# Attention and a gated feed-forward layer on one core: five of seven score slots transposed by DMA, q loaded in 1 KB packets, sums inverted before they are transposed

## The chip, the core and the metric

The kernel runs on one core of a Trainium2 chip. Its engines are TensorE (PE, with its weight loads shown as PEld), VectorE (DVE), ScalarE (ACT), GpSimd (POOL) and SyncE (SP), which here issues every DMA; 16 DMA engines move the data. The metric is device time in microseconds. Three runs of the kernel before gave a median of 922.18 us (921.71 to 923.18). A difference of 0.2% (1.8 us) is about what such a measurement can tell from no change.

## The reference

Eight batches of twelve heads, 448 tokens, head size 64. `q` and `k` are normalised by their root mean square and a gain, then come softmax attention and, per batch, a feed-forward layer: a 768 to 1024 product, relu, a convolution over three neighbouring tokens, a sigmoid gate, and a 1024 to 768 product.

```python
    q_n, k_n = (rmsnorm(q, g_q), rmsnorm(k, g_k))
    scores = scale * np.matmul(q_n, k_n.transpose(0, 1, 3, 2))
    scores = scores - np.max(scores, axis=-1, keepdims=True)
    attn = np.exp(scores)
    attn = attn / (np.sum(attn, axis=-1, keepdims=True) + 1e-09)
    return np.matmul(attn, v).astype(np.float32)
    ...
    h = np.maximum(x @ w_in, 0.0)
    for k in range(K):
        conv_out += conv_w[k][None, None, :] * hp[:, k:k + S, :]
    gate = 1.0 / (1.0 + np.exp(-conv_out))
    return (h * gate @ w_out).astype(np.float32)
```

## The kernel before

The work is cut into 48 **pairs** of heads, six to a batch. A pair has 2 x 448 = 896 query rows, cut into seven **slots** of 128; slot 3 lies across both heads. For a pair, q, k and v come in by one DMA each (`load_k`, `load_q`, `v_load`). Squares, their sums (`square`, `square_sum`) and a Newton iteration (`rsqrt`) give the norms, `apply_rms` applies them. K is turned by PE and split into two fp16 halves (`qk_transpose`, `qk_hi`, `qk_lo`); q likewise up to pair 7 and by a DMA transpose from pair 8 on (`x_cast`, `x_rest`, `x_turn`).

Scores (`scores`, L600) are three fp16 products of the halves for each slot. Slots are computed in `GROUPS`: two slots of different heads go side by side on the two halves of PE's rows (`HALF`), the slot across both heads takes the whole array with a masked copy of q (`qz`). `soft_max` (DVE, L604) and `soft_exp` (ACT, L614) give the unnormalised powers `e` and, as an accumulator, the row sums `rsum`.

The powers P have to be turned before they meet v. There are two ways. On the **raw** way four fp32 transposes on PE (`p_transpose`, L651) put a slot into PSUM, `p_evac` (a copy that shows as L78) brings it to `PT`, and `pv` multiplies it in fp32 with `v` (L723). On the **cast** way `p_hi` and `p_lo` split the slot into two fp16 halves in one of three buffers `ph`, `p_turn` (L643) is a DMA transpose into `PT`, and `pv` multiplies in fp16 with the split v, `vp`, in three products (L732). `nd(n)` is the number of slots on the cast way: none up to pair 7, four (slots 0, 6, 1, 5) from pair 8 on.

v is scaled by a power of two per batch (`v_scaled`, L696, in place, for every pair), then cast (`v_hi`, `v_lo`). The row sums go `sum_transpose` (PE, L666), `sum_evac` (DVE, L671, adds 1e-9), `sum_inverse` (DVE, L663, a reciprocal of 7 x 128), `sum_store` to DRAM (SP, L676) and two `sum_load`s (SP, L682), one for each head, which spread a head's 448 values over 64 partitions of `rB`. `x_scale` (DVE, L741) multiplies the product in PSUM with `rB`, and `x_hi` and `x_lo` split it into the fp16 halves `x` of the feed-forward layer. Once a batch has its six pairs, `in_part` (L806), `in_relu`, `in_conv`, `in_tanh`, `in_gate`, `in_hi`, `in_lo` and `out_part` (L883) follow, interleaved with the next batches' attention.

**What sets the order.** Every step is planned with a due time (`at`), and a planner lays the steps out before the program is built. It knows for each step which engines may do it and an assumed cost (`options`), what it needs (`needs`), how many buffers there are (`BUFS`), and picks step after step by the earliest start and the due time. `PH` holds the due times' parameters and the extra delay that a second choice of engine has to beat. The result is one fixed order on each engine, and an instruction that waits holds up everything behind it on its engine. So any edit to costs, steps or `PH` moves nearly every instruction. In the first 150 us or so the weights are also loaded, converted and split (`convert`, L210 to L218, `split`, `rest`).

Of the kernel before, what the change touches and what calls it, by code (L numbers as in the profile page):

```python
# [49 lines left out]
def tile_attention_moe(ctx: ExitStack, tc, q, k, v, g_q, g_k, w_in, conv_w, w_out, out):  # L50
# [41 lines left out]
    def move(e, dst, src):  # L92
# [10 lines left out]
        rB=2, vacc=2, vsc=4, cwb=3, s=4, t=2, m=4, rd=2, rsum=2, rT=2, mx=10, ph=3, vp=2,  # L103
# [60 lines left out]
    warm = const.tile([P, 1], F32, name="warm")  # L164

# [401 lines left out]
    SLOTS = (0, 6, 1, 5, 2, 4, 3)  # L567
    GROUPS = ((0, 1), (2, 3), (4, 5), (6,))
# [4 lines left out]
    def nd(n):  # L573
        return 0 if n < PH["n1"] else 2 * PH["dg"]
# [14 lines left out]
    def scores(n, g):  # L589
# [29 lines left out]
    def inside(n, j):

        return PH["ein"] and j < nd(n)

    def powers(n, j):
        return bank("s", (n, j))[:, :S] if inside(n, j) else old("e", (n, j))

    def p_hi(n, j):
# [28 lines left out]
    def p_evac(n, j):  # L655
        c = SLOTS[j] - nd(n) // 2
# [4 lines left out]

    def sum_inverse(n):
        nc.vector.reciprocal(old("rT", n), old("rT", n))  # L663
# [6 lines left out]
    def sum_evac(n):  # L670
        nc.vector.tensor_scalar(  # L671
            new("rT", n, [NS, P], F32), bank("t", ("r", n))[:NS, :P], 1e-9, None, op0=ALU.add
# [5 lines left out]
    def sum_load(n, h):  # L678
        if h == 0:
            new("rB", n, [P, S], F32)  # L680
        row = old("rd", n).rearrange("t p -> (t p)")[h * S : (h + 1) * S]
        queue("rb").dma_start(  # L682
            old("rB", n)[HALF[h]], row.unsqueeze(0).to_broadcast([64, S])
# [7 lines left out]
    def pvs(n):  # L691
        return (*range(0, NB, PV_STEP), *(range(NB, NB + 3) if nd(n) else ()))

    def v_scaled(n):
        v = old("v", n).rearrange("p h t d -> p (h t d)")
        elementwise(on["v_scaled", n]).tensor_scalar(  # L696
            v, v, old("vsc", n // NP)[:PB, 1:2], None, op0=ALU.mult
        )
# [38 lines left out]
    def x_place(n):  # L737
        return bank("m", ("v", n))[:, :S] if PH["xin"] else old("rB", n)

    def x_scale(n):  # L740
        nc.vector.tensor_tensor(x_place(n), bank("m", ("v", n))[:, :S], old("rB", n), op=ALU.mult)  # L741

    def x_hi(n):
        copy(on["x_hi", n], new("x", n, [P, 2, S], F16)[:, 0], x_place(n))

    def x_lo(n):
        xt = old("x", n)
        binary(on["x_lo", n], xt[:, 1], x_place(n), xt[:, 0], ALU.subtract)

    def plan_attention(n):  # L750
# [197 lines left out]
    def prepare():  # L948
# [3 lines left out]
        nc.vector.memset(ones, 1.0)  # L952
# [605 lines left out]
```

## Time and profile before

| | |
|---|---|
| median of three runs | 922.18 us (921.71 to 923.18) |
| the profiled execution, its own time | 925.0 us |
| its span in the trace | 923.2 us |
| mean granted TensorE clock | 0.972 |
| PE busy | 849.0 us |
| DVE busy | 730.2 us |
| ACT busy | 667.4 us |
| POOL busy | 627.3 us |
| DMA queue, share of 16 engines | 62.1% |

Busy time of an engine is the time in which at least one of its instructions runs. Matmuls are pipelined and overlap in the trace, so what a group of them costs is read from where the next group starts. The other 1.8 us of the profiled execution lie outside the span. DMA-issuing instructions are not counted as busy time of SP.

### The profile page before, as it was taken

How to read it: one execution, taken by the hardware profiler on the slowest of the kernel's cores; microseconds unless marked ns; L12 is line 12 of the kernel's file. 1: busy time of each engine (PE TensorE's matmuls, PEld its weight loads, DVE VectorE, ACT ScalarE, POOL GpSimd, SP SyncE). 2: the span in 40 equal slices, each digit the busy share in tenths (PEclk: the TensorE clock that was granted, in tenths of full speed). 3: DMA queues.
4: the chain of work that ended last, by engine and by line, in shares of the span. 5: the costliest groups of instructions: out<-in, count | busy, mean ns of one | idle time of the engine just before them, and what ended most of it. 6: DMA issues, size and time to landing. Idle time of an engine off the chain costs nothing.

```text
span 923.2 us, 18519 instructions
## 1 busy us (share of the span) xinstructions
PE 849.0 (92%) x6430; PEld 508.7 (55%) x6430; DVE 730.2 (79%) x1336; ACT 667.4 (72%) x1525; POOL 627.3 (68%) x705
## 2 busy tenths in 40 slices
PE   1686687998999999999999999999999999999998
PEld 0343344555656566556665566566655666566554
DVE  6998987999788887798798976898789876893330
ACT  3677776887688776788688877787788867885441
POOL 2396887787699768668688857777778755872120
PEclk9897787999999999999999999999999999999999
DMA  8934432376885878556976588568696695455001
GB/s 212 259 96 126 122 113 63 89 135 117 185 147 130 156 152 170 123 117 124 187 148 139 115 182 168 95 135 164 150 170 126 119 175 120 84 94 112 18 18 52
DMA packets 296878, 120.18 MB, mean 130 GB/s; under 512 B 258048, under 2 KB 293200, under 8 KB 296784
## 3 DMA queue, kind: packets, MB, share of 16 engines
q1 hardware_dynamic: 296784, 119.00, 62.1%
q8 instruction: 50, 0.82, 0.4%
q14 instruction: 44, 0.36, 0.1%
HBM read 56.65 MB, written 11.18 MB: 73 GB/s over the span
## 4 chain that ended last, share of the span: by engine, by line
PE 67%; DVE 18%; DMA 5%; ACT 4%; issue 2%; SPq 2%; POOL 2%; DVEq 0%; ACTq 0%; POOLq 0%
PE bank L883 19%; PE bank L806 19%; PE bank L600 9%; PE bank L723 7%; PE bank L651 6%; PE bank L732 4%; DMA rB<-rd 3%; PE bank L462 2%; DVE rT L663 1%; DMA v<-in_v_dram 1%; DVE st L365 1%; DVE wo L214 1%; POOL sq L90 1%; DVE vacc L528 1%; SPq L643 1%
## 5 line engine op out<-in xcount | busy, mean ns | idle before, releaser
L806 PE MATMUL bank<-x,wi 128*128 128x448 f16 x1152 | 241.9, 354 | 0.3 <-ACT e_(8_0_1731 L614 0.3
L883 PE MATMUL bank<-wo,gring 128*128 128x384 f16 (+1 forms) x1056 | 205.4, 327 | 0.7 <-DVE c_(4_7_8185 L839 0.3
L806 PEld LDWEIGHTS <-wi 128*128 128x128 f16 x1152 | 110.2, 98 | 99.8 <-issue 14.7
L883 PEld LDWEIGHTS <-gring 128*128 128x128 f16 (+1 forms) x1056 | 101.8, 99 | 62.7 <-issue 11.0
L78 ACT COPY PT<-bank 112x512 f32<-112x512 f32 x166 | 96.6, 586 | 42.9 <-PE bank L651 41.9
L600 PE MATMUL bank<-kT,qT 64*128 64x448 f16 x864 | 107.1, 370 | 1.2 <-ACT qT L78 0.6
L90 POOL TENSOR_TENSOR sq<-qkf,st 112x512 f32<-112x512 f32 x79 | 87.5, 1125 | 17.6 <-DVE st L387 15.6
L723 PE MATMUL bank<-PT,v 112*64 112x192 f32 (+1 forms) x768 | 88.8, 374 | 1.7 <-ACT PT L78 1.3
L90 POOL TENSOR_TENSOR x<-rB,x 128x448 f16<-128x448 f32 x48 | 51.5, 1073 | 47.5 <-ACT x L78 36.4
L723 PEld LDWEIGHTS bank<-PT,v 112*64 112x64 f32 x768 | 51.5, 138 | 34.5 <-issue 18.1
L600 PEld LDWEIGHTS <-qT 64*128 64x128 f16 x864 | 34.8, 97 | 49.4 <-issue 28.2
L365 DVE TENSOR_REDUCE st<-sq 112x16 f32<-112x1024 f32 x48 | 57.9, 1207 | 3.7 <-ACT sq L357 3.6
L732 PE MATMUL bank<-PT,vp 112*64 112x256 f16 x960 | 59.2, 273 | 0.0
L696 POOL TENSOR_SCALAR v<-v,vsc 112x512 f32<-112x512 f32 x35 | 57.6, 1649 | 1.9 <-DVE vsc L200 0.9
L732 PEld LDWEIGHTS <-vp 112*64 112x64 f16 x960 | 53.0, 110 | 2.6
L741 DVE TENSOR_TENSOR rB<-bank,rB 128x448 f32<-128x448 f32 x48 | 29.7, 619 | 29.4 <-DMA rB<-rd 20.7
L491 POOL COPY qz<-qT 64x128 f16<-64x128 f16 x88 | 33.2, 378 | 28.3 <-DMA qT<-qkf 17.2
L462 PE MATMUL bank<-ident,sq 112*128 112x112 f32 x224 | 33.6, 276 | 18.8 <-POOL sq L90 18.7
L90 POOL TENSOR_TENSOR vp<-v,vp 112x512 f16<-112x512 f32 x39 | 46.6, 1195 | 2.8 <-ACT vp L78 1.6
L883 PE MATMUL bank<-wo,wi 128*128 128x384 f16 (+1 forms) x192 | 46.9, 326 | 0.0
L663 DVE RECIPROCAL rT<-rT 7x128 f32<-7x128 f32 x48 | 44.9, 935 | 0.7
L90 POOL TENSOR_TENSOR qkf<-sq,qkf 112x512 f16<-112x512 f32 x29 | 35.0, 1208 | 13.8 <-ACT qkf L78 7.2
(2235 smaller groups left out, 2101.6 us busy)
## 6 DMA issues: line engine op xcount, KB each, us to landing
qkf<-in_k_dram SPq DMA_DIRECT2D x48, 224.0 KB
qkf<-in_q_dram SPq DMA_DIRECT2D x48, 224.0 KB
v<-in_v_dram SPq DMA_DIRECT2D x48, 224.0 KB
rB<-rd SPq DMA_DIRECT2D x96, 112.0 KB
wo<-in_moe_w_in_dram SPq DMA_DIRECT2D x12, 512.0 KB
gring<-in_moe_w_out_dram SPq DMA_DIRECT2D x16, 384.0 KB
PT<-ph SPq DMA_TRANSPOSE x160
rd<-rT SPq DMA_DIRECT2D x48, 3.5 KB
```

Of the source, the lines that this page charges most:

```text
L78: (nc.scalar.copy if e == "ACT" else elementwise(e).tensor_copy)(dst, src)
L90: elementwise(e).tensor_tensor(dst, a, b, op=op)
L365: nc.vector.tensor_reduce(old("st", m)[:, 0, n - m].rearrange("p i s -> p (i s)"), old("sq", n).rearrange("p i h t d -> p (i h t) d"), axi ...
L462: nc.tensor.transpose(ps[:, t * PB : (t + 1) * PB], x[:, t], ident[:PB, :PB])
L600: nc.tensor.matmul(ps[u][:, :S], lhs, kt[r, w], start=(i == 0), stop=(i == 2))
L651: nc.tensor.transpose(ps[:PB, kt * P : (kt + 1) * P], e[:, kt * PB : (kt + 1) * PB], ident)
L663: nc.vector.reciprocal(old("rT", n), old("rT", n))
L696: elementwise(on["v_scaled", n]).tensor_scalar(v, v, old("vsc", n // NP)[:PB, 1:2], None, op0=ALU.mult)
L723: nc.tensor.matmul(ps[HALF[h], out[h]], v[:, h, k], pt[:, k, col[h]], start=(k == 0), stop=(k == NB - 1),)
L732: nc.tensor.matmul(ps[HALF[h], out[h]], v[:, w, h, k], pt[:PB, a, k, col[h]], start=(i == 0 and k == 0), stop=(i == 2 and k == NB - 1),)
L806: nc.tensor.matmul(ps[:, :S], wi[:, wl, c, fc * P : (fc + 1) * P], old("x", b * NP + c)[:, xl], start=(i == 0), stop=(i == 3 * NP - 1),)
L883: nc.tensor.matmul(ps[p0 : p0 + m, :NO2], g, wo[:, wl, fc, half * NO2 : (half + 1) * NO2], start=(i == 0), stop=(i == 3 * NFC - 1),)
```

## The change

1. **Five slots by DMA from pair 10 on.** `nd` is 5 from pair 10 on and 0 before. Slots 1 to 5 go the cast way, and slots 0 and 6, the first of the one head and the last of the other, the raw way. The slot across both heads is now one of the cast ones and is computed as the third group instead of the fourth.
2. **q in another order.** `load_q` reads four neighbouring tokens into one partition, 1 KB in a piece, as `load_k` does. The scores' rows, P's columns and the sums come out in that order, and `x_scale` puts them back: it writes a new tile `xs` with a step of four elements. `rB` is free after `x_scale`.
3. **v's scale in its cast.** `v_scaled` is gone. `v_hi` casts and scales in one instruction (ACT or DVE), `v_lo` is a scalar_tensor_tensor, on DVE alone. The raw way uses v unscaled; the scale is multiplied into the inverted sums of the raw slots in `sum_evac`, by a column of `vsc` that `v_scale` fills with the scale for raw slots and 1 for cast ones.
4. **Sums inverted, then transposed.** `sum_add` (ACT, DVE or POOL) and `sum_inverse` (DVE) work on 128 x 7; then come the transpose and `sum_evac` with the scale. One `sum_load` takes the place of two: its source pattern counts 2 heads, 64 copies of step 0, 448 elements.
5. **Planner.** `PH` has other numbers, some assumed costs are changed, POOL may also do `x_cast`, `x_hi`, `in_hi` and `p_hi`; switches that were off (`xin`, `gin`, `ein`) are removed.

```diff
 PH = dict(
-    T0=18.19, N0=5, T=16.2, ti=26.722, si=4.889, so=6.734, hop=0.568, beta=0.028, wi0=-41.512,
+    T0=16.073, N0=7, T=15.869, ti=26.722, si=4.889, so=6.416, hop=0.568, beta=0.028, wi0=-40.836,
...
     def load_q(n):
-            old("qkf", n)[:, 0], qf[rows].rearrange("(h t p) d -> p h t d", h=2, t=NB)
+            old("qkf", n)[:, 0], qf[rows].rearrange("(h p t) d -> p h t d", h=2, t=NB)
...
     def v_scale(b):
+        nc.vector.scalar_tensor_tensor(
+            sc[:NS, 6:7], raw_slot[:NS], sc[:NS, 1:2], cast_slot[:NS], op0=ALU.mult, op1=ALU.add
+        )
...
-    SLOTS = (0, 6, 1, 5, 2, 4, 3)
-    GROUPS = ((0, 1), (2, 3), (4, 5), (6,))
+    SLOTS = (2, 4, 1, 5, 3, 0, 6)
+    GROUPS = ((0, 1), (2, 3), (4,), (5, 6))
     def nd(n):
-        return 0 if n < PH["n1"] else 2 * PH["dg"]
+        return 0 if n < PH["n1"] else PH["dg"]
...
     def sum_inverse(n):
-        nc.vector.reciprocal(old("rT", n), old("rT", n))
+        nc.vector.reciprocal(old("rsum", n), old("rsum", n))
...
     def sum_evac(n):
-        nc.vector.tensor_scalar(
-            new("rT", n, [NS, P], F32), bank("t", ("r", n))[:NS, :P], 1e-9, None, op0=ALU.add
+        w = 6 if nd(n) else 1
+        copy_scaled(
+            on["sum_evac", n], new("rT", n, [NS, P], F32), bank("t", ("r", n))[:NS, :P],
+            old("vsc", n // NP)[:NS, w : w + 1],
         )
...
-    def sum_load(n, h):
-        if h == 0:
-            new("rB", n, [P, S], F32)
-        row = old("rd", n).rearrange("t p -> (t p)")[h * S : (h + 1) * S]
+    def sum_load(n):
+        rows = old("rd", n).rearrange("t p -> (t p)").rearrange("(h s) -> h s", h=2)
         queue("rb").dma_start(
-            old("rB", n)[HALF[h]], row.unsqueeze(0).to_broadcast([64, S])
+            new("rB", n, [P, S], F32),
+            rows.unsqueeze(1).to_broadcast([2, 64, S]),
         )
...
-    def v_scaled(n):
-        elementwise(on["v_scaled", n]).tensor_scalar(
...
     def v_lo(n):
-        binary(on["v_lo", n], vp[:, 1], old("v", n), vp[:, 0], ALU.subtract)
+        nc.vector.scalar_tensor_tensor(
+            vp[:, 1], old("v", n), old("vsc", n // NP)[:PB, 1:2], vp[:, 0], op0=ALU.mult,
+            op1=ALU.subtract,
+        )
...
     def x_scale(n):
-        nc.vector.tensor_tensor(x_place(n), bank("m", ("v", n))[:, :S], old("rB", n), op=ALU.mult)
+        by_load = lambda t: t.rearrange("m (t p) -> m t p", t=NB)
+        nc.vector.tensor_tensor(
+            new("xs", n, [P, S], F32).rearrange("m (p t) -> m t p", t=NB),
+            by_load(bank("m", ("v", n))[:, :S]), by_load(old("rB", n)), op=ALU.mult,
+        )
...
-            sum_load=lambda: [dma("rb", 0.4)],
+            sum_load=lambda: [dma("rb", 0.75)],
```

How the order changes is shown at three places. Names in the rows carry the pair: `PT_24` is P of pair 24, `rd_28` the sums of pair 28.

**PE, where the turned P of pair 24 meets v, before.** L806 is the feed-forward layer, L723 the fp32 product, L732 the fp16 one, which goes on after the last row to 24 matmuls.

```order
L806 LDWEIGHTS wi32_77
L806 MATMUL bank4_5934<-x_18_4585,wi32_77 128x448
L723 MATMUL bank3_5942<-PT_24_5721,v_24_4093 64x192 x8
L732 LDWEIGHTS vp_24_5767
L732 MATMUL bank3_5942<-PT_24_5721,vp_24_5767 64x256
L732 LDWEIGHTS vp_24_5767
L732 MATMUL bank3_5942<-PT_24_5721,vp_24_5767 64x256
```

**The same place in the change.** L816 is the feed-forward layer, L732 the fp32 product, L606 the scores.

```order
L816 LDWEIGHTS wi32_77
L816 MATMUL bank3_5871<-x_18_4547,wi32_77 128x448
L732 MATMUL bank1_5881<-PT_24_5667,v_24_4047 64x128 x8
L606 LDWEIGHTS qz1_74
L606 MATMUL bank5_5896<-kT_25_5673,qz1_74 128x448
L606 LDWEIGHTS qz1_74
L606 MATMUL bank5_5896<-kT_25_5673,qz1_74 128x448
```

The fp32 product has 128 columns instead of 192. The fp16 one, 24 matmuls of 320 columns instead of 256, no longer follows it at once: scores of pair 25 and feed-forward work stand between. Over the whole program PE changes 346 times instead of 298 between the whole array, split rows (two slots side by side) and split columns (L723 and L732 before, 64-row outputs).

**SP, around the sums of pair 28, before.** L643 is `p_turn`, L453 `x_turn`, L676 `sum_store`, L682 `sum_load`, L897 a store of the result.

```order
L643 DMA_TRANSPOSE PT_28_6733<-ph2_72 128x8x128
L676 DMA rd_28_6946<-rT_28_6896 7x128
L643 DMA_TRANSPOSE PT_29_6962<-ph0_70 128x8x128
L682 DMA rB_28_6982<-rd_28_6946 64x448
L453 DMA_TRANSPOSE qT_30_7004<-qkf_30_6299 128x8x112
L643 DMA_TRANSPOSE PT_29_6962<-ph1_71 128x8x128
L682 DMA rB_28_6982<-rd_28_6946 64x448
```

**The same place in the change** (L684 `sum_store`, L688 `sum_load`, L641 `p_turn`, L456 `x_turn`).

```order
L684 DMA rd_28_6863<-rT_28_6840 7x128
L641 DMA_TRANSPOSE PT_28_6619<-ph1_71 128x8x128
L688 DMA rB_28_6905<-rd_28_6863 128x1x448
L641 DMA_TRANSPOSE PT_29_6921<-ph2_72 128x8x128
L456 DMA_TRANSPOSE qT_30_6938<-qkf_30_6188 128x8x112
L905 DMA out_0_dram<-c_('o'_3_0_1_6874 128x384
L641 DMA_TRANSPOSE PT_29_6921<-ph0_70 128x8x128
```

There is one load of the inverted sums where there were two with two transposes between them, and pair 29 has five `p_turn`s instead of four.

**DVE, from the inverse of the sums of pair 24 on, before.** L604 is `soft_max`, L696 `v_scaled`, L671 `sum_evac`.

```order
L696 TENSOR_SCALAR v_26_4561<-v_26_4561,vsc_4_5484 112x512
L671 TENSOR_SCALAR rT_24_5907<-bank3_5895 7x128
L663 RECIPROCAL rT_24_5907<-rT_24_5907 7x128
L604 TENSOR_REDUCE sst_(25_0_5920<-bank6_5899 128x1
L604 TENSOR_REDUCE sst_(25_1_5929<-bank5_5900 128x1
```

**The same place in the change** (L668 `sum_inverse`, L711 `v_lo`, L610 `soft_max`).

```order
L668 RECIPROCAL rsum_24_5622<-rsum_24_5622 128x7
L711 SCALAR_TENSOR_TENSOR vp_25_5759<-v_25_4324,vsc_4_5447,vp_25_5759 112x512
L610 TENSOR_REDUCE sst_(25_0_5858<-bank7_5839 128x1
L610 TENSOR_REDUCE sst_(25_1_5869<-bank4_5840 128x1
L610 TENSOR_REDUCE sst_(25_2_5879<-bank6_5847 128x1
```

The evacuation of the sums left DVE (all 48 are on ACT now), the reciprocal works on seven elements a partition instead of 128, and `v_lo` came to DVE (38 instructions; 39 were on POOL and one on DVE).

More of the change, by code (lines that the diff above doesn't have):

```diff
@@ L611, in soft_exp @@
         c = SLOTS[j]
-        if not inside(n, j):
-            new("e", (n, j), [P, S], F32)
         nc.scalar.activation(
-            powers(n, j), bank("s", (n, j))[:, :S], AF.Exp, bias=old("sst", (n, j)),
+            new("e", (n, j), [P, S], F32), bank("s", (n, j))[:, :S], AF.Exp, bias=old("sst", (n, j)),
             accum_out=old("rsum", n)[:, c : c + 1],
         )
[L619 to L624, printed above, removed]
     def p_hi(n, j):
@@ L764, in plan_attention @@
         s += NS * d
+        at(s + 2.0, sum_add, n)
+        at(s + 2.3, sum_inverse, n)
         at(s + 2.6, sum_transpose, n)
         at(s + 3.2, sum_evac, n)
-        at(s + 3.6, sum_inverse, n)
         at(s + 4.0, sum_store, n)
-        for h in range(2):
-            at(s + 6.0, sum_load, n, h)
-        at(s - 6.0, v_scaled, n)
+        at(s + 6.0, sum_load, n)
         if nd(n):
@@ L1114, in needs @@
             yield "soft_exp", *back(n, a[1], 1)
-            if not inside(n, a[1]):
-                m, j = back(n, a[1], 1)
-                left_ = BUFS["e"] - 1
-                while left_ or inside(m, j):
-                    left_ -= not inside(m, j)
-                    m, j = back(m, j, 1)
-                yield ("p_lo" if j < nd(m) else "p_transpose"), m, j
+            m, j = back(n, a[1], BUFS["e"])
+            yield ("p_lo" if j < nd(m) else "p_transpose"), m, j
             yield "sum_transpose", n - BUFS["rsum"]
@@ L1185, in needs @@
             yield "pv", n, pvs(n)[-1]
-            for h in range(2):
-                yield "sum_load", n, h
+            yield "x_lo", n - BUFS["xs"]
+            yield "sum_load", n
         elif name == "x_hi":
@@ L1332, in tile_attention_moe @@
         x_cast="qh", x_rest="ql", apply_gain="rms", qk_hi="hi", apply_rms="rms", x_hi="x", x_lo="lo", in_hi="g", in_lo="g", q_middle="qz", in_carry="g",
-        out_evac="ev", v_scaled="vs", v_hi="hi", v_lo="lo", p_hi="ph", p_lo="pl", v_bound="v", rest="w", rsqrt="rs", square="sq", convert="w", in_relu="relu", in_conv="cv", p_evac="evac",
+        out_evac="ev", sum_evac="ev", sum_add="sa", v_hi="hi", p_hi="ph", p_lo="pl", v_bound="v", rest="w", rsqrt="rs", square="sq", convert="w", in_relu="relu", in_conv="cv", p_evac="evac",
     )
@@ L1339, in takes @@
         if name == "scores":
[L1340 removed]
+            return "s", [((a[0], j), ("soft_exp", a[0], j)) for j in GROUPS[a[1]]]
         if name == "qk_transpose":
@@ L1402, in mode @@
     def mode(name, *a):
-        return name if name == "pv" or name == "scores" and a[1] < NG - 1 else ""
+        return name if name == "pv" or name == "scores" and a[1] != 2 else ""
     taken = {step: takes(*step) for step in steps}
@@ L1432, in tile_attention_moe @@
     SHARED = (
-        "apply_rms", "apply_gain", "x_cast", "x_rest", "p_lo", "p_hi", "v_lo", "v_hi", "v_scaled",
+        "apply_rms", "apply_gain", "x_cast", "x_rest", "p_lo", "p_hi", "v_lo", "v_hi", "sum_add",
         "x_hi", "x_lo", "in_hi", "in_lo", "in_carry", "q_middle", "convert", "rest", "moe_scales", "rsqrt",
     )
-    shared = set(SHARED)
-    for key, names in dict(xin=("x_hi", "x_lo"), gin=("in_hi", "in_lo"), ein=("p_hi", "p_lo")).items():
-        if PH[key]:
-            shared -= set(names)
     port = dict(DVE=0.0, POOL=0.0)
     def locks(e, name):
-        return e == "POOL" or e == "DVE" and name in shared
+        return e == "POOL" or e == "DVE" and name in SHARED
     BULK = ("load", "load_k", "load_q", "v_load")
```

160 lines of the change are left out of this document (86 added, 74 removed).

## The prediction

> **What bounds the kernel now.** I read the page's busy times first, then busy time by stretches, then PE's timeline in the middle, then the waits.
>
> ```profile
> PE 849.0 (92%) x6430; PEld 508.7 (55%) x6430; DVE 730.2 (79%) x1336; ACT 667.4 (72%) x1525; POOL 627.3 (68%) x705
> PE 67%; DVE 18%; DMA 5%; ACT 4%; issue 2%; SPq 2%; POOL 2%; DVEq 0%; ACTq 0%; POOLq 0%
> ```
>
> PE is busiest and has two thirds of the chain that ended last; DVE has most of the rest. The stretches (span, then busy time of PE, PEld, DVE, ACT, POOL, granted clock, DMA share, GB/s) say where:
>
> ```profile
> 0.00:50.00 50.00, 22.11 (x101) 12.36 (x103) 39.64 (x85) 24.68 (x55) 18.19 (x40) 0.90 0.95 225
> 50.00:100.00 50.00, 38.59 (x247) 20.18 (x244) 45.62 (x84) 37.90 (x94) 40.55 (x39) 0.90 0.42 113
> 100.00:150.00 50.00, 34.64 (x185) 18.36 (x185) 45.10 (x82) 35.07 (x85) 43.02 (x43) 0.74 0.39 109
> 150.00:200.00 50.00, 49.07 (x312) 25.98 (x309) 46.03 (x78) 41.83 (x91) 39.71 (x44) 0.95 0.42 83
> 200.00:250.00 50.00, 45.15 (x363) 28.41 (x363) 43.66 (x86) 37.52 (x88) 36.30 (x37) 1.00 0.75 151
> 400.00:450.00 50.00, 47.03 (x383) 29.60 (x382) 44.75 (x86) 39.65 (x92) 34.00 (x37) 1.00 0.74 147
> 500.00:550.00 50.00, 48.60 (x440) 30.59 (x440) 41.45 (x79) 39.98 (x93) 35.03 (x37) 1.00 0.73 153
> 550.00:600.00 50.00, 50.00 (x389) 30.52 (x386) 37.96 (x68) 37.02 (x84) 38.50 (x49) 1.00 0.72 137
> 200.00:850.00 650.00, 636.00 (x5135) 392.62 (x5134) 537.32 (x986) 503.89 (x1159) 476.52 (x533) 1.00 0.71 140
> ```
>
> Up to 150 us DVE is 79 to 91% busy while PE idles 55 us in all and is granted less than its full clock (0.74 to 0.90). From 200 to 850 us PE runs at full clock and idles 14 us in 650, in a few stretches (4.9 us, 3.0, 1.4) where DVE is busiest. So two stages have two limits: the start goes by DVE, the long middle by PE.
>
> **PE's work.** Its timeline (start, time, what), one row of the start of the program last:
>
> ```profile
> 500.21 1.52 PE L723 MATMUL bank<-PT,v 112*64 112x192 f32 x16
> 501.56 1.48 PE L732 MATMUL bank<-PT,vp 112*64 112x256 f16 x24
> 502.97 0.74 PE L600 MATMUL bank<-kT,qT 64*128 64x448 f16 x6
> 503.65 1.88 PE L806 MATMUL bank<-x,wi 128*128 128x448 f16 x9
> 505.93 0.60 PE L651 MATMUL bank<-ident,e_(27_4_6555 128*112 128x128 f32 x4
> 506.36 1.30 PE L806 MATMUL bank<-x,wi 128*128 128x448 f16 x6
> 509.71 1.31 PE L600 MATMUL bank<-kT,qT 64*128 64x448 f16 x12
> ...
> 134.96 3.23 PE L723 MATMUL bank<-PT,v 112*64 112x448 f32 x16
> 138.12 0.60 PE L462 MATMUL bank<-ident,sq 112*128 112x112 f32 x4
> ```
>
> From start to next start, a slot's four transposes take 506.36 - 505.93 = 0.43 us, the fp32 product 1.35 us at 192 columns and 3.16 us at 448, the fp16 one 1.41 us at 256. Two points give 7.1 ns a column, so 0.90 us at 128 columns. The weight loads of that product bound it from below:
>
> ```profile
> 400.00:600.00 200.00, 18.26 (x192) 12.71 (x192) 1.00 0.73 147
> 400.00:600.00 200.00, 21.81 (x144) 17.04 (x144) 1.00 0.73 147
> ```
>
> (the fp32 product and the transposes alone, same columns with PE and PEld only). 12.71 us for 192 loads are 66 ns each, 16 of them 1.06 us. I take 1.0 us, 0.35 less than now. The fp16 product at 320 columns takes 320/256 x 1.41 = 1.76, 0.35 more. The two cancel, and a pair saves one slot's transposes: 38 x 0.43 = **-16.3 us**. Pairs 8 and 9 lose the cast way: 4 x 0.43 + (3.16 - 1.35) - 1.41 = 2.1 each, **+4.2** (twice that at a lower clock). A change of array shape costs what six split-row matmuls take before the whole array follows (503.65 - 502.97 = 0.68) beyond six more of their kind (1.31 - 0.74 = 0.57): 0.11 us, and 48 more of them make **+5.3**. PE in sum: **-7 us**, between -16 (fp32 product at 0.90, switches free) and 0 (1.06, pairs 8 and 9 twice as dear).
>
> **The other engines.** Groups by line and shape (count, busy us, mean ns):
>
> ```profile
> L663 DVE RECIPROCAL rT<-rT 7x128 f32<-7x128 f32 x48 | 44.9, 935 | 0.7
> L671 DVE TENSOR_SCALAR rT<-bank 7x128 f32<-7x128 f32 x48 | 13.2, 274 | 16.0 <-PE bank L666 15.9
> L696 POOL TENSOR_SCALAR v<-v,vsc 112x512 f32<-112x512 f32 x35 | 57.6, 1649 | 1.9 <-DVE vsc L200 0.9
> L90 POOL TENSOR_TENSOR vp<-v,vp 112x512 f16<-112x512 f32 x39 | 46.6, 1195 | 2.8 <-ACT vp L78 1.6 <-PE bank L651 0.9
> L480 DVE SCALAR_TENSOR_TENSOR kT<-bank,G,kT 128x448 f16<-128x448 f32 x48 | 32.5, 677 | 9.8 <-ACT kT L82 9.4
> L301 DVE SCALAR_TENSOR_TENSOR wo<-wo,wsc 128x768 f16<-128x768 f32 x8 | 9.6, 1203 | 1.7 <-ACT wo L293 1.6
> L741 DVE TENSOR_TENSOR rB<-bank,rB 128x448 f32<-128x448 f32 x48 | 29.7, 619 | 29.4 <-DMA rB<-rd 20.7 <-PE bank L732 8.4
> L90 DVE TENSOR_TENSOR sq<-qkf,st 112x512 f32<-112x512 f32 x17 | 15.6, 928 | 0.0
> L78 ACT COPY PT<-bank 112x512 f32<-112x512 f32 x166 | 96.6, 586 | 42.9 <-PE bank L651 41.9
> L78 DVE COPY PT<-bank 112x512 f32<-112x512 f32 x10 | 6.8, 679 | 0.0
> ```
>
> *DVE.* The inverse on 7 elements a partition isn't in the trace: 7/128 of 935 ns is 0.05 us, the 274 ns row (short, same shape) the other end; I take 0.15: 48 x (0.935 - 0.15) = -38. The sums' evacuation leaves: -13. `v_lo` comes, 38 x 0.75 = +29 (between L480's 0.68 and two thirds of L301, 0.80). Ten `apply_rms` (0.928) go to POOL: -9. Together -31, and -45 with the smaller ones (`v_scaled`, `p_evac`, `p_lo`). `x_scale` with its step of four is unmeasured: no dearer (0.619), or twice that, +30 on DVE. I take the first, as the same elements pass.
>
> [...] No row here has such a step.
>
> *ACT* gains the evacuation of sums and most of `sum_add` and loses 26 copies of P (-15): about even. *POOL* loses 57.6 + 46.6, gains 37 `p_lo`, 32 casts, the ten `apply_rms`, squares and half of a weight's split: about even. At a pair in 16.7 us (144 transposes in 200 us are 36 slots, 12 pairs) ACT is 80% and POOL 70% busy in the 500 us row, so both cover what they get. If that cover went, each added 0.6 us instruction on ACT would cost a pair that much.
>
> **DMA and SP.** SP's queue and two waits:
>
> ```profile
> 527.95 0.28 SPq L676 DMA_DIRECT2D rd<-rT  x1
> 530.21 1.24 SPq L643 DMA_TRANSPOSE PT<-ph  x1
> 531.54 0.54 SPq L682 DMA_DIRECT2D rB<-rd  x1
> 534.83 0.59 SPq L682 DMA_DIRECT2D rB<-rd  x1
> ...
> DVE rB L741 <- DMA rB<-rd: 20.7, 15, 6.0
> ACT ph L78 <- DMA PT<-ph: 6.8, 8, 1.9
> ...
> rB<-rd SPq DMA_DIRECT2D x96, 112.0 KB
> ```
>
> A pair adds a `p_turn` (1.24 us of SP) and drops a load (0.59): with six transposes and six or seven issues of about 0.5 SP spends some 11 of 16.7 us issuing. The transpose's 256 KB cost each of 16 engines 16 KB; at 153 GB/s and a share of 0.73 an engine moves 13.1 GB/s, so 1.2 us a pair. q's 896 pieces become 224, which costs nothing more and may save about that. A share of 0.73 leaves room, and the three `ph` buffers make ACT wait 6.8 us in all now. I take 0; each us by which a `p_turn` lands later than the next but two slot's cast would stand on ACT, with the next powers behind it.
>
> **The start.** Up to `x_scale` of pair 7, DVE's order lacks 8 inverses (-6.3), 8 evacuations (-2.2), 5 copies of P (-3.4) and 6 of the 8 `wo` rests (-7.2; four are POOL's now, two come later): 19 us of some 176. Half of it shows, I think, as the chain there alternates between DVE and PE: **-9**, between 0 and -19. Of the middle's 14 us of idle PE time, a DVE with less to do gives back **-4**, I think, between 0 and -8.
>
> **Sum.** The profiled execution took 925.0 us: -7 - 9 - 4 = -20, 905. It lies 2.8 above the median of 922.2, so on the median's footing **902 us**; own range 884 to 918 (all the terms' good ends together would give 879, all the bad ones 922).
>
> **Rivals.** *One: the load of the sums gets narrow.* Already 15 `x_scale`s wait for `rB`, with the next pair's `soft_max` behind them on DVE, and ACT's powers behind those. The one load spares the second issue, which came 3.3 us after the first. But its source counts 2, 64, 448 instead of 64, 448. If a transfer is shared out by its first count, two engines move the 224 KB: 115 KB each, 7.7 us at 14.8 GB/s (225 GB/s, share 0.95) to 8.8 at 13.1, against 1.1 on sixteen. Some 7 us late, less 3.3, less DVE's idle time (8.55 of 50 us, 2.9 a pair) leaves 1 us a pair, some 40 us: 945. Those two engines would also carry 0.73 x 16.7 + 7 + 1.2 = 20 us a pair, where a pair is to take 16.3, with every `p_turn` behind them: 1060 if they set the pace. It decides from the point where the load takes over some 6 us; I put it at 970. For it: the 15 waits. Against: PE's order now has feed-forward work and scores ahead of the fp16 product, so that `x_scale` stands later, and at a share of 0.95 in the first 50 us the same engines moved 225 GB/s, so that 0.73 is not their limit.
>
> [...] No row of this trace shows a transfer's engines.
>
> *Two: the gain is hidden.* PE's saving is met by waits for later fp16 products or for `v_lo` on DVE, and the start keeps its pace as ACT or POOL take over (POOL is 86% busy from 100 to 150 us). Then the PE and middle terms and half of the start go: 922 - 4 = 918, and 915 to 926 with one wait more or less; about 920.
>
> *Three: the start gains whole.* DVE's 19 us all show, and PE's and the middle's better ends (-16, -8) come with them: 922 - 43 = 879.
>
> **Chances.** Forecast 0.52, narrow load 0.25, hidden 0.15, start whole 0.08. Faster by over 0.2% (below 920.3): 0.50 + 0.08 + 0.07 = 0.65; slower (above 924.0): 0.24 + 0.04 = 0.28; within, 0.07. The range takes in the bounds of the forecast, the hidden gain and the nearer part of the narrow load, and leaves out some 0.05 below and 0.14 above: 884 to 955.
>
> **What would show it.** PE: 146 slots' transposes at 0.43 us, the fp32 product near 1.0, the fp16 one near 1.76 us. Start: more PE busy time up to 150 us than the 95 us of now, at a higher granted clock. Narrow load: long waits of `x_scale` and of `p_hi` on DMA, and 1792-byte packets on a DMA share that falls while DVE waits. I am wrong if PE idles over 30 us from 200 to 850 us, if the first 150 us hold no more PE work, or if `x_scale` takes 1.2 us.

## The result, and the profile after

| | before | the change |
|---|---|---|
| median | 922.68 us (921.71 to 925.58, 4 runs) | **1034.3 us** (1030.65 to 1037.52, 4 runs) |
| profiled execution, span | 925.0, 923.2 us | 1037.52, 1035.7 us |
| mean granted TensorE clock | 0.972 | 0.946 |

The ratio is 1.1203, with an interval of 1.1157 to 1.1248: 12% slower. The forecast was 902, the range ended at 955. What came is the mechanism of rival One, the narrow load, at a higher price than I gave it.

The page of the changed kernel: busy times, the DMA queue, and the chain that ended last by engine and by line.

```profile
PE 876.9 (85%) x6262; PEld 489.9 (47%) x6262; DVE 707.5 (68%) x1272; ACT 673.3 (65%) x1592; POOL 618.0 (60%) x750
q1 hardware_dynamic: 294768, 126.86, 72.9%
DMA 35%; PE 23%; ACT 12%; DVE 11%; POOL 10%; issue 6%; SPq 1%; ACTq 0%; POOLq 0%; DVEq 0%
DMA PT<-ph 23%; DMA rB<-rd 8%; PE bank L891 8%; PE bank L816 5%; POOL ph L90 3%; PE bank L606 3%; PE bank L649 3%; POOL sq L90 3%; PE bank L732 2%; ACT ph L78 2%; DVE xs L749 1%; DMA v<-in_v_dram 1%; SPq L641 1%; DVE st L368 1%; PE bank L741 1%
```

PE had 67% of the chain, and has 23%. DMA had 5% and has 35%, and most of that is not the load of the sums (`rB<-rd`, 8%) but the transposes of P (`PT<-ph`, 23%). The waits (who waits for whom: us in all, times, longest):

```profile
ACT ph L78 <- DMA PT<-ph: 104.4, 33, 6.0
POOL ph L90 <- ACT ph L78: 104.0, 65, 6.1
DVE xs L749 <- DMA rB<-rd: 90.1, 32, 5.4
```

ACT waited 6.8 us for a free `ph` before, now 104.4; `x_scale` waited 20.7 us for `rB`, now 90.1. To see where in the program the time goes, I cut it at three starts of `x_scale`: those of pair 7, pair 10 (the first with five cast slots) and pair 47. First the kernel before, then the change (columns as in the prediction):

```profile
0.00:185.26 185.26, 129.68 (x720) 68.42 (x721) 162.02 (x302) 126.89 (x294) 128.32 (x144) 0.86 0.54 135
185.26:237.82 52.56, 48.83 (x386) 29.75 (x384) 47.18 (x87) 42.52 (x100) 42.39 (x51) 1.00 0.70 131
237.82:855.38 617.56, 607.28 (x4921) 375.12 (x4920) 504.50 (x924) 474.54 (x1090) 447.29 (x502) 1.00 0.71 140
```

```profile
0.00:178.31 178.31, 124.59 (x709) 64.28 (x710) 146.52 (x289) 121.80 (x299) 104.23 (x131) 0.89 0.52 137
178.31:236.64 58.33, 55.48 (x372) 29.96 (x369) 48.81 (x81) 45.73 (x108) 48.09 (x54) 1.00 0.56 84
236.64:968.70 732.06, 634.31 (x4780) 360.56 (x4781) 495.27 (x879) 482.29 (x1144) 456.38 (x557) 0.95 0.86 132
```

Up to pair 10 the change is 1.2 us ahead. From there to pair 47 it takes 732.1 us instead of 617.6, that is 19.8 us a pair instead of 16.7, and PE idles 98 us of it instead of 10. Its granted clock falls from 1.00 to 0.95 there. Against the kernel before, the loss is all in the stretch in which five slots of P go by DMA.

How wide a load is can be seen at pair 47, where little else is left to move. SP's queue, and the mean share (in tenths) and rate of the 16 DMA engines from 961 to 969 us in slices of 0.2 us:

```profile
961.36 0.52 SPq L688 DMA_DIRECT2D rB<-rd  x1
961.97 0.44 SPq L905 DMA_DIRECT2D out_dram<-c_('o'_6_1_1_11403  x1
```

```profile
DMA  0899999413993111111102011111101115993110
GB/s 4 173 215 215 212 204 198 90 27 128 374 399 139 45 45 45 54 45 54 36 18 27 9 27 54 45 54 54 54 36 54 54 54 200 365 384 108 46 54 31
```

Up to 962.4 us some 210 GB/s pass, and two stores of 192 KB go at up to 399 and 384 GB/s. Between and behind these is a long stretch at mostly 36 to 54 GB/s and a share of one tenth, up to the end of the window: it fits a load whose 224 KB go over a small part of the engines. Two of sixteen would show as 0.125, and this tail agrees with that.

No view of the profile names a transfer's engines, but the trace keeps the times at which each transfer's semaphore is stepped; I take the last step for its landing. The loads of the kernel before step theirs 16 times each. All 48 loads of the changed kernel step theirs three times: once about 1 us after the issue, and twice at the end (for this one at 968.25 and 968.31 us). Of the store issued behind it at 961.97, 14 steps come by 963.91 us and the last two at 968.75 and 968.82, right behind the load's. So I read one late step as one engine, and the load as sitting on two of sixteen. Its 128 packets of 1792 bytes run for 5.9 us, on average 2.0 of them at a time, and it lands 7.6 us after its issue (medians of the 48).

In the middle SP itself is held up (start, time, what):

```profile
509.04 0.53 SPq L688 DMA_DIRECT2D rB<-rd  x1
509.67 0.44 SPq L349 DMA_DIRECT2D qkf<-in_k_dram  x1
510.20 3.11 SPq L641 DMA_TRANSPOSE PT<-ph  x1
513.42 0.52 SPq L524 DMA_DIRECT2D v<-in_v_dram  x1
513.99 0.45 SPq L353 DMA_DIRECT2D qkf<-in_q_dram  x1
514.53 4.61 SPq L641 DMA_TRANSPOSE PT<-ph  x1
```

Issuing these two `p_turn`s behind the load takes 3.11 and 4.61 us; the median of the kernel before is 1.26. Over 2 us take 65 of 190 here, and 10 of 160 before.

### The profile page after: what moved, and what is told of

It reads as the page before. It is cut to its first block, busy times and chain, and to the rows that moved or that the text cites. A ratio compares the mean times of both kernels' runs of the same rounds, so it can differ in the third digit from the quotient of the medians.

```text
span 1035.7 us, 18206 instructions
## 1 busy us (share of the span) xinstructions
PE 876.9 (85%) x6262; PEld 489.9 (47%) x6262; DVE 707.5 (68%) x1272; ACT 673.3 (65%) x1592; POOL 618.0 (60%) x750
## 4 chain that ended last, share of the span: by engine, by line
DMA 35%; PE 23%; ACT 12%; DVE 11%; POOL 10%; issue 6%; SPq 1%; ACTq 0%; POOLq 0%; DVEq 0%
DMA PT<-ph 23%; DMA rB<-rd 8%; PE bank L891 8%; PE bank L816 5%; POOL ph L90 3%; PE bank L606 3%; PE bank L649 3%; POOL sq L90 3%; PE bank L732 2%; ACT ph L78 2%; DVE xs L749 1%; DMA v<-in_v_dram 1%; SPq L641 1%; DVE st L368 1%; PE bank L741 1%
## 5 line engine op out<-in xcount | busy, mean ns | idle before, releaser
L816 PE MATMUL bank<-x,wi 128*128 128x448 f16 x1152 | 248.2, 360 | 0.0
L816 PEld LDWEIGHTS <-wi 128*128 128x128 f16 x1152 | 111.4, 99 | 100.4 <-issue 16.5
L606 PE MATMUL bank<-kT,qT 64*128 64x448 f16 x864 | 117.3, 387 | 12.8 <-DVE xs L749 3.3
L749 DVE TENSOR_TENSOR xs<-bank,rB 128x448 f32<-128x448 f32 x48 | 46.1, 961 | 115.5 <-DMA rB<-rd 90.1
L90 POOL TENSOR_TENSOR sq<-qkf,st 112x512 f32<-112x512 f32 x89 | 99.6, 1138 | 6.6 <-DVE st L390 4.5
L78 ACT COPY PT<-bank 112x512 f32<-112x512 f32 x140 | 81.4, 584 | 23.2 <-PE bank L649 22.7
L90 POOL TENSOR_TENSOR x<-xs,x 128x448 f16<-128x448 f32 x48 | 51.1, 1064 | 67.5 <-ACT x L78 61.2
L732 PE MATMUL bank<-PT,v 112*64 112x128 f32 (+1 forms) x768 | 76.8, 341 | 0.5 <-ACT PT L78 0.5
L741 PE MATMUL bank<-PT,vp 112*64 112x320 f16 x912 | 71.8, 305 | 5.9 <-DMA PT<-ph 5.9
L606 PEld LDWEIGHTS <-qT 64*128 64x128 f16 x864 | 36.6, 100 | 72.6 <-issue 48.5
L732 PEld LDWEIGHTS bank<-PT,v 112*64 112x64 f32 x768 | 43.3, 138 | 30.9 <-issue 20.0
L90 POOL TENSOR_TENSOR sq<-qkf 112x1024 f32<-112x1024 f32 x27 | 51.6, 1913 | 6.6 <-issue 6.3
L78 ACT CAST x<-xs 128x448 f16<-128x448 f32 x37 | 20.8, 563 | 47.1 <-DVE xs L749 45.1
L465 PEld LDWEIGHTS bank<-ident,sq 112*128 112x128 f32 x224 | 25.7, 147 | 31.7 <-POOL sq L90 23.2
L90 POOL TENSOR_TENSOR qkf<-sq,qkf 112x512 f16<-112x512 f32 x27 | 33.1, 1226 | 10.3 <-ACT qkf L78 9.8
```

Of the source, the lines that this page charges most:

```text
L78: (nc.scalar.copy if e == "ACT" else elementwise(e).tensor_copy)(dst, src)
L90: elementwise(e).tensor_tensor(dst, a, b, op=op)
L465: nc.tensor.transpose(ps[:, t * PB : (t + 1) * PB], x[:, t], ident[:PB, :PB])
L606: nc.tensor.matmul(ps[u][:, :S], lhs, kt[r, w], start=(i == 0), stop=(i == 2))
L732: nc.tensor.matmul(ps[HALF[h], out[h]], v[:, h, k], pt[:, k, col[h]], start=(k == 0), stop=(k == NB - 1),)
L741: nc.tensor.matmul(ps[HALF[h], out[h]], v[:, w, h, k], pt[:PB, a, k, col[h]], start=(i == 0 and k == 0), stop=(i == 2 and k == NB - 1),)
```

## The experiments

My theory after the result: the source's outermost count, 2, puts the single load on two DMA engines, and these carry the transposes' share too, so that the transposes come late. Rivals: one large load in place of two is itself the cause; the step of four in `x_scale` or the five cast slots are; or `x_scale` only gets its factor late, with the transposes not to blame.

**Two loads in the changed kernel.** Each reads one head's row, with counts 64 and 448. All engines keep their order otherwise.

```diff
-        queue("rb").dma_start(
-            new("rB", n, [P, S], F32),
-            rows.unsqueeze(1).to_broadcast([2, 64, S]),
-        )
+        t = new("rB", n, [P, S], F32)
+        for h in range(2):
+            queue("rb").dma_start(t[HALF[h]], rows[h].unsqueeze(0).to_broadcast([64, S]))
```

> The changed kernel with the sums loaded by two DMAs of 64 rows again (source counts 64, 448), in the same place; every engine's order is otherwise the same. Narrow-load theory: the whole loss is the load on two of 16 DMA engines, so the time falls from 1034 to 895 to 915, the waits of x_scale for rB fall from 90 us to under 25, ACT's wait for P's transposes from 104 us to under 15. Rival (the fifth transpose a pair, or x_scale at 0.96 and v_lo at 0.97 us on DVE, is the cause): it stays over 980.

Measured: **895.33 us** (890.02 to 898.38, 4 runs), ratio to before 0.9693 (0.9657 to 0.9728). This one edit is worth 139 us. Page and waits of this kernel:

```profile
PE 831.0 (94%) x6262; PEld 476.7 (54%) x6262; DVE 704.4 (79%) x1272; ACT 674.7 (76%) x1592; POOL 620.3 (70%) x750
PE 63%; DVE 14%; POOL 9%; ACT 5%; DMA 4%; issue 3%; SPq 0%; POOLq 0%; ACTq 0%; DVEq 0%
```

```profile
ACT ph L78 <- DMA PT<-ph: 16.8, 23, 2.1
DVE xs L749 <- DMA rB<-rd: 3.8, 5, 1.0
```

Time and `x_scale`'s wait came as expected; ACT's wait is 16.8 us, a little above the 15 expected, but a sixth of what it was. PE sets the pace again. The two kernels' landings show what the load did to P's transposes. In the changed kernel 70 of the 190 were issued while a load of the sums was under way, and they landed a median of 7.5 us after their issue; the other 120 took 3.2. All 62 that took over 6 us were among the 70, and each of them landed at least 0.9 us after the load. With two loads none of 190 took over 6 us. Everything else in the change together is therefore a gain of some 3%.

**One load in the kernel before.** The same source of 2, 64, 448, in one load, and nothing else.

```diff
     def sum_load(n, h):
         if h == 0:
-            new("rB", n, [P, S], F32)
-        row = old("rd", n).rearrange("t p -> (t p)")[h * S : (h + 1) * S]
-        queue("rb").dma_start(
-            old("rB", n)[HALF[h]], row.unsqueeze(0).to_broadcast([64, S])
-        )
+            rows = old("rd", n).rearrange("t p -> (t p)").rearrange("(h s) -> h s", h=2)
+            queue("rb").dma_start(
+                new("rB", n, [P, S], F32), rows.unsqueeze(1).to_broadcast([2, 64, S])
+            )
```

> The kernel before with one load of the sums (source counts 2, 64, 448) in the place of its first load, and nothing in the place of the second; all else as before. Narrow-load theory: two engines move all of it there too, 980 to 1040, with waits of x_scale for rB over 60 us. Rival: one load instead of two costs nothing by itself, within 1% of 922.

Measured: 1029.45 us (1025.13 to 1033.77), ratio 1.1132 (1.1068 to 1.1196). Its waits:

```profile
ACT ph L78 <- DMA PT<-ph: 100.2, 29, 5.7
DVE rB L740 <- DMA rB<-rd: 49.6, 31, 8.3
```

The load alone does it, with four cast slots and no step in `x_scale`: none of the other parts is needed. The time is in the range expected; `x_scale`'s wait, 49.6 us, is less than the 60 expected, and ACT's for P's transposes is the larger one.

**The count, dose by dose.** Two loads of the same bytes, but the rows stored c times, so that the source counts c, 64/c, 448. Shown for c = 4; 2, 8 and 16 differ by that number.

```diff
     def sum_store(n):
-        queue("rd").dma_start(new("rd", n, [NS, P], F32, pD), old("rT", n))
+        rd = new("rd", n, [4, NS, P], F32, pD)
+        queue("rd").dma_start(
+            rd.rearrange("c t p -> t c p"),
+            old("rT", n).unsqueeze(1).to_broadcast([NS, 4, P]),
+        )
...
     def sum_load(n):
...
+        rows = old("rd", n).rearrange("c t p -> c (t p)").rearrange("c (h s) -> c h s", h=2)
+        t = new("rB", n, [P, S], F32)
+        for h in range(2):
+            queue("rb").dma_start(
+                t[HALF[h]], rows[:, h].unsqueeze(1).to_broadcast([4, 64 // 4, S])
+            )
```

> The changed kernel with two loads of 64 rows whose source counts 4, 16, 448 (the sums are stored in four copies to make the count real). If the first count sets the number of engines, four of them carry 28 KB of each half: some 4 us a pair instead of 8, on four engines whose load is then some 16.5 us a pair, near a pair's time: 910 to 960. If only a count of 2, or the single DMA, is bad: as with two plain loads, 895 to 915.

> As the one with a count of 4, but the sums are stored in 16 copies and the source counts 16, 4, 448. If the first count sets the number of engines: as with two plain loads within 1%. If three counts in the source, or the stored copies, are what costs: as slow as the count of 4 or slower.

> Two loads, as before, but the source's counts are 2, 32, 448 (the rows stored twice): the bytes, the number of loads and their issues are those of the two-load version. If the outermost count sets how many DMA engines carry a load, each load sits on two engines and it is as slow as the single load, 1000 to 1040 us. If it was the joining of two loads into one that cost the time, it stays near 895.

> Two loads with the source's counts 8, 8, 448 (the rows stored eight times). By the outermost count eight engines carry each load; between 923 us at a count of 4 and 893 at 16 it should lie at 890 to 905 us. If the count is not what matters and the stored copies cost the time at count 4, it lies above 900.

| first count of the two loads | median us | ratio to before | ACT's wait for `PT<-ph` |
|---|---|---|---|
| 2 | 1040.53 (1039.32 to 1041.74) | 1.1269 (1.1233 to 1.1304) | 103.5 us |
| 4 | 923.24 (916.32 to 927.32) | 0.9969 (0.9939 to 1.0) | 43.8 us |
| 8 | 896.87 (896.46 to 897.28) | 0.9713 (0.9685 to 0.9741) | 23.5 us |
| 16 | 892.56 (891.86 to 893.26) | 0.9652 (0.962 to 0.9683) | 20.0 us |
| 64 (first experiment) | 895.33 (890.02 to 898.38) | 0.9693 (0.9657 to 0.9728) | 16.8 us |

At a count of 2 two loads are as slow as one (just above the 1000 to 1040 expected), so that joining two loads is not the cause; the count is. The other three came within their ranges, and the extra copies cost nothing that shows, as 16 of them give the lowest median. From 8 on the count costs next to nothing, and 16 and 64 agree within their intervals. The late steps of each load's semaphore are 2, 4, 8, 16 and 16 at these five counts, in every one of the 96 loads: what follows the count shows in the steps too, not only in the times. The last pair's loads at counts 2 (966 to 976 us) and 4 (850 to 860 us), slices of 0.25 us:

```profile
DMA  5999950001299220100020049811111111110000
GB/s 106 218 208 210 202 105 0 7 22 50 75 350 377 80 57 7 14 7 14 14 36 7 29 156 381 309 50 50 50 50 50 50 49 49 49 49 0 0 0 0
```

```profile
DMA  8999920020149823022222207930000000000000
GB/s 161 211 213 214 194 46 0 0 29 36 57 166 333 307 85 65 29 86 93 100 99 102 92 25 301 369 117 0 0 0 0 0 0 0 0 0 0 0 0 0
```

The plateaus are 50 GB/s at a share of 1 and about 100 GB/s at 2, which makes some 25 GB/s an engine if two and four engines carry them. At count 2 the two loads together (50 GB/s) move hardly faster than the single load did (36 to 54), as if both sat on the same two engines. Which of the engines they are is not in the trace.

**The load that nobody reads.** The changed kernel with its narrow load, but `x_scale` multiplies by a constant: the division by the sums is left out.

```diff
...
     def x_scale(n):
...
-            by_load(bank("m", ("v", n))[:, :S]), by_load(old("rB", n)), op=ALU.mult,
+            by_load(bank("m", ("v", n))[:, :S]), even.unsqueeze(2).to_broadcast([P, NB, PB]), op=ALU.mult,
```

> The changed kernel with its one narrow load still issued, but nobody reads it: x_scale multiplies by a constant (the division by the sums is left out). Clogging theory: the two engines are full and hold up P's transposes, so the time stays at 985 to 1035. Lateness theory: the loss is x_scale's own wait with DVE behind it, so it falls under 930.

Measured: 1020.25 us (1017.91 to 1022.59), ratio 1.1031 (1.0998 to 1.1063). Its longest wait on DMA:

```profile
ACT ph L78 <- DMA PT<-ph: 130.3, 40, 5.6
```

With no one waiting for the load, 125 of the 139 us (1020.25 - 895.33) are still lost. The lateness of `rB` itself is worth the other 14 us or so; what costs is the load standing in the way of other transfers, P's transposes above all. The lateness shows most ahead of pair 10, where no P goes by DMA: `x_scale` of pair 10 starts at 236.6 us in the changed kernel, at 224.1 with the load unread and at 212.4 with two loads (one profiled execution each), and up to there `x_scale` waits 18.7 us for `rB` in the changed kernel. So the narrow load costs 24 us at the start too, hidden in the first profile by the lead of 1.2 us over the kernel before.

**`x_scale`'s step.** Two kernels with two loads. One multiplies without a step (putting the tokens back is left out); one reads PSUM and `rB` with a step of 112 elements and writes without a gap.

```diff
     def x_scale(n):
-        by_load = lambda t: t.rearrange("m (t p) -> m t p", t=NB)
...
-            new("xs", n, [P, S], F32).rearrange("m (p t) -> m t p", t=NB),
-            by_load(bank("m", ("v", n))[:, :S]), by_load(old("rB", n)), op=ALU.mult,
+            new("xs", n, [P, S], F32),
+            bank("m", ("v", n))[:, :S], old("rB", n), op=ALU.mult,
```

```diff
     def x_scale(n):
-        by_load = lambda t: t.rearrange("m (t p) -> m t p", t=NB)
+        by_token = lambda t: t.rearrange("m (t p) -> m p t", t=NB)
...
-            new("xs", n, [P, S], F32).rearrange("m (p t) -> m t p", t=NB),
-            by_load(bank("m", ("v", n))[:, :S]), by_load(old("rB", n)), op=ALU.mult,
+            new("xs", n, [P, S], F32).rearrange("m (p t) -> m p t", t=NB),
+            by_token(bank("m", ("v", n))[:, :S]), by_token(old("rB", n)), op=ALU.mult,
```

> Two loads, and x_scale writes without a step (putting the tokens back in order is left out). If the step of four made x_scale 0.98 instead of 0.62 us: back to 0.62, DVE 17 us less busy. If PE bounds the middle: only the start shortens, 889 to 894 against 895. If DVE bounds the middle too: 875 to 885.

> Two loads, and x_scale puts the tokens back by reading PSUM and rB with a step of 112 elements and writing without one. If the step on the written side is the price: 0.62 to 0.70 us, and 889 to 894. If a step on any side, or the inner run of four, costs as much: 0.9 us or more, and 893 to 897.

Measured: 890.93 us without a step, ratio 0.9645 (0.9614 to 0.9675); 895.25 us with stepped reads, ratio 0.9678 (0.9664 to 0.9693). The groups, first of the two-load kernel, then of these two:

```profile
L749 DVE TENSOR_TENSOR xs<-bank,rB 128x448 f32<-128x448 f32 x48 | 47.0, 979 | 31.5 <-PE bank L741 27.0 <-DMA rB<-rd 3.8 <-PE bank L732 0.6
L711 DVE SCALAR_TENSOR_TENSOR vp<-v,vsc,vp 112x512 f16<-112x512 f32 x38 | 36.5, 960 | 0.1
L668 DVE RECIPROCAL rsum<-rsum 128x7 f32<-128x7 f32 x48 | 9.3, 195 | 12.1 <-ACT rsum L663 7.5 <-POOL rsum L665 4.5
```

```profile
L749 DVE TENSOR_TENSOR xs<-bank,rB 128x448 f32<-128x448 f32 x48 | 29.7, 618 | 28.9 <-PE bank L741 24.9 <-DMA rB<-rd 2.6 <-PE bank L732 1.3
```

```profile
L749 DVE TENSOR_TENSOR xs<-bank,rB 128x448 f32<-128x448 f32 x48 | 44.0, 917 | 30.5 <-PE bank L741 25.3
```

The step costs 0.36 us an instruction (0.979 against 0.618) on the writing side and 0.30 on the reading side. Without the step that is 17 us less DVE work for about 4 us of median, with intervals that overlap: DVE has the room.

**The inverse first, in the kernel before.** 1e-9 is added and the inverse taken on 128 x 7, ahead of the transpose.

```diff
     def sum_inverse(n):
-        nc.vector.reciprocal(old("rT", n), old("rT", n))
+        r = old("rsum", n)
+        nc.vector.tensor_scalar(r, r, 1e-9, None, op0=ALU.add)
+        nc.vector.reciprocal(r, r)
...
     def sum_evac(n):
-        nc.vector.tensor_scalar(
-            new("rT", n, [NS, P], F32), bank("t", ("r", n))[:NS, :P], 1e-9, None, op0=ALU.add
-        )
+        nc.vector.tensor_copy(new("rT", n, [NS, P], F32), bank("t", ("r", n))[:NS, :P])
```

> The kernel before with one part of the change: 1e-9 added and the sums inverted on 128 x 7, ahead of the transpose. DVE loses 48 x 0.7 us = 34 us. Start theory: the first 150 us go by DVE, so 5 to 12 us are gained, 912 to 918. Rival: PE's order sets the start too, within 0.2% of the kernel before.

Measured: 915.22 us (913.88 to 916.25), ratio 0.9894 (0.988 to 0.9909), a gain of 1.1%. Its stretch from pair 10 to pair 47:

```profile
236.22:846.25 610.03, 608.00 (x4934) 376.69 (x4933) 502.52 (x952) 473.96 (x1092) 456.18 (x519) 1.00 0.71 142
```

It takes 610.0 us instead of 617.6, and PE idles 2 us of it instead of 10. Pair 10 comes 1.6 us earlier, pair 7 even 3.5 us later (188.8 us). So in these profiled executions the inverse pays in the middle, not at the start. The time lies in the range expected, but the theory behind that range was the start; that it came so is luck.

**Two more things tried on the two-load kernel.** One casts from pair 8 on (`n1=8` for `n1=10`), the other tells the planner of two issues:

```diff
-            sum_load=lambda: [dma("rb", 0.75)],
+            sum_load=lambda: [dma("rb", 0.4, 2)],
```

> Two loads of the sums' rows, and the cast path (five slots of P by DMA) from pair 8 on instead of from pair 10 on. If the forecast's term for pairs 8 and 9 is right (4.2 us of PE work given away by starting two pairs later), this is some 4 us under the two-load version: 888 to 893 us. If the start is bound by DVE or ACT there, or if the two more casts hold up POOL while it still helps with the start, it stays within 2 us of 895 or goes above it.

> Two loads of the sums' rows, and the planner is told of two issues on SP's queue where it counted one, so that it may place the steps behind them differently. If the orders of before suit the two loads already, 893 to 898 us, no change from 895; if the second issue's place matters, as far down as 888.

Measured: 898.35 us, ratio 0.9723 (0.9696 to 0.9751), for the cast from pair 8; 900.31 us, ratio 0.9759 (0.9733 to 0.9784), for the planner. Neither beats 895.33: the interval of the first overlaps with that of the two-load kernel (0.9657 to 0.9728), the second's lies just above it. The planner's 900.31 is above both of the ranges expected. The stretches of the kernel with two loads, and those from pair 7 to 10 and from 10 to 47 with the cast from pair 8:

```profile
0.00:160.14 160.14, 116.57 (x701) 61.30 (x702) 145.16 (x288) 120.88 (x297) 106.07 (x131) 0.95 0.53 153
160.14:212.39 52.25, 52.25 (x360) 29.24 (x360) 45.35 (x82) 45.85 (x109) 48.60 (x54) 1.00 0.43 96
212.39:821.20 608.81, 599.72 (x4802) 351.06 (x4799) 497.03 (x879) 484.54 (x1145) 456.34 (x557) 1.00 0.77 159
```

```profile
164.46:221.49 57.03, 51.66 (x374) 28.65 (x373) 53.46 (x91) 47.95 (x109) 48.96 (x54) 0.94 0.58 120
221.49:825.88 604.39, 596.12 (x4784) 349.38 (x4784) 494.40 (x885) 483.35 (x1143) 456.99 (x548) 1.00 0.78 160
```

With the cast from pair 8 the stretch from pair 7 to 10 is 4.8 us longer, not 4.2 shorter: DVE is 53.5 of 57.0 us busy in it, and PE idles 5.4. The next stretch gives 4.4 us back, and pair 7 starts 4.3 later. So work moved from one stretch to another, and what the two casts cost by themselves isn't shown; the 4.2 us were not gained.

## Why the prediction was wrong

**The step that failed is the term for DMA and SP ("I take 0")**, and with it the choice of the forecast over rival One. In its place the runs show 139 us, the price of a load whose source counts 2 first (1034.3 against 895.33). I had the source's counts, what they would come to on two engines, and the waits that would show it, and put it at 0.25. Two arguments turned me from it. The first was that a share of 0.73 leaves room. That share is a mean over 16 engines and says nothing about two of them. The second was that `x_scale` stands later in PE's new order, so that a late load is covered; that is about the wrong instruction, as the load that nobody reads showed.

**Rival One's price.** That a transfer is shared out by its first count was a supposition, with no row of the kernel before to show it. The runs agree with it: 2, 4, 8, 16 and 16 late steps at counts of 2, 4, 8, 16 and 64. So its condition held, and its size was not right. I had given two bounds: 945 if only `x_scale` is late, 1060 if the two engines set the pace at 20 us a pair. The measured pace is 19.8 us a pair and the time 1034.3, near the upper bound, and 970 between them had no mechanism behind it. That the sum 0.73 x 16.7 + 7 + 1.2 = 20.4 comes so near is partly luck. The load's packets run for 5.9 us, not 7, by which the sum is 19.3. And it counts the work of two engines, while the late transposes step their semaphores all 16 times within 0.15 us (median of the 62, at most 1.6): they come late as a whole, not by their share on two engines. The load holds up P's transposes issued behind it (7.5 us from issue to landing, against 3.2 for the others); why all sixteen steps come late isn't shown. The long waits that I named as signs came, and PE idled 87 us from 200 to 850 us, where over 30 was to show me wrong. One sign was wrong: the DMA share did not fall but rose, from 0.71 to 0.86.

**The rest of the forecast** can be judged on the kernel with two loads, 895.33 us against the 902 forecast. Its profiled execution took 890.02 us, 5 under its median and 35 less than before's 925.0, where my terms gave 20. Between the medians of runs on one chip, 924.01 and 895.33, it is 29.

| stretch | forecast | measured, two loads | |
|---|---|---|---|
| start to pair 7 | -9 (0 to -19) | 160.1 - 185.3 = **-25.1** | better than its better end |
| pairs 7 to 10 | +4.2 | 52.25 - 52.56 = **-0.3** | PE's work right in kind (+3.4); its idle time fell by 3.7 |
| 10 to 47, PE busy | -15.9 + 5.2 = -10.7 | 599.7 - 607.3 = **-7.6** | right in kind, 3 too much |
| 10 to 47, PE idle | -4 (0 to -8) | 9.1 - 10.3 = **-1.2** | inside its bounds; -4.9 with pairs 7 to 10 |

(37 of the 38 pairs: 37 x 0.43 us saved, and 37/38 of the 5.3 us for changes of shape.) *PE's durations* came as worked out. Its timeline in the two-load kernel:

```profile
501.72 1.09 PE L732 MATMUL bank<-PT,v 112*64 112x128 f32 x16
502.75 0.74 PE L606 MATMUL bank<-kT,qT 64*128 64x448 f16 x6
505.48 1.82 PE L741 MATMUL bank<-PT,vp 112*64 112x320 f16 x24
507.23 0.34 PE L891 MATMUL bank<-wo,gring 128*128 128x384 f16 x1
508.54 0.60 PE L649 MATMUL bank<-ident,e_(29_5_7018 128*112 128x128 f32 x4
508.98 0.33 PE L891 MATMUL bank<-wo,gring 128*128 128x384 f16 x1
```

From start to start the fp32 product takes 1.03 us (1.0 taken), the fp16 one 1.75 (1.76) and a slot's transposes 0.44 (0.43). The 1.06 us of weight loads, by which the prediction bounded the fp32 product from below, was a little too high as a bound.

*The start* is where the forecast was too small. PE's work up to pair 7 has about as many matmuls (701 against 720) and takes 13.1 us less, at a granted clock of 0.95 instead of 0.86: 129.68 x 0.86 / 0.95 = 117.4 if its time goes by the clock, against 116.57 measured. The other 12 us are idle time. I had let half of DVE's 19 us show and not reckoned that PE's own work gets quicker with it. Which part of the change brings it isn't settled: the inverse alone didn't (pair 7 came 3.5 us later, pair 10 1.6 us earlier), and q in 1 KB packets and the moved `wo` rests weren't tried apart.

*Pairs 8 and 9* I priced by PE's work, and that part was near: 52.25 - 48.83 = 3.4 us more of it against 4.2. But PE had idled 3.7 us in this stretch before, and with two loads it idles none, so that the stretch didn't get longer. The forecast's -4 for the idle time stood for the whole middle, these pairs too, and there -4.9 came.

*DVE's prices.* The inverse takes 0.195 us (0.15 taken), `v_lo` 0.960 (0.75), `x_scale` 0.979 (0.619). The last two add 38 x 0.21 + 48 x 0.36 = 25 us of DVE work. Of `x_scale`'s part some 4 us show. I had taken the step as free, with a factor of 2 as the dear case; by the rows it costs a factor of 1.6 (0.979 against 0.618). In the middle the inverse by itself took PE's idle time from 10 to 2 us; the whole change left it at 9, so that something in the rest gave most of that back. What did isn't shown.

## What to carry to other kernels

Before joining two DMAs into one, look at the outermost count of the patterns: here a 2 in place of a 64 in the source's cost 139 us on 895, with the same bytes and one issue fewer. Look for the harm in the transfers issued behind it and not only in the load's own reader (with nobody reading it, 125 of the 139 us were still lost), and do not take a mean share over 16 engines for room on two of them. And when a mechanism is worked out with a lower and an upper bound, ask which resource fills up, instead of taking a value between.

## What was not expected of the hardware

- From pair 10 to pair 47 the mean DMA share is higher in the slow kernel (0.86) than in the one with two loads (0.77), while it moves less (132 against 159 GB/s). The share adds up the packets' times, and these are long in the slow kernel: its 256-byte packets took 35.7 ns on average, those of the kernel before 24.2 in the same stretch. Here it is no measure of what is moved.
- Of the 230 DMA transposes (P's and q's), 72 took SP over 2 us to issue in the slow kernel, up to 4.7, and 12 with two loads, up to 2.4: the jam reaches back to the engine that issues.
- One narrow load delays the transposes of P issued behind it: the 70 behind one landed 7.5 us after their issue (median), the other 120 took 3.2.
- The reciprocal on 128 x 7 takes 0.195 us and on 7 x 128 takes 0.935, for the same number of elements.
